# The q and k loads of an attention and MLP kernel moved from SyncE's DMA queue to GpSimd's, and two raw weight loads asked for at an earlier place

## The chip, the cores and the metric

One NeuronCore of a Trainium2 chip runs the whole program. The metric is device time in microseconds of one execution, as the median of three runs. The profile that is read below comes from one more execution, with the hardware profiler on, and its own time stands in the table beside its span.

## What is computed

The reference, cut to what matters:

```python
# q, k, v: (4, 12, 448, 64) fp32; cap: a scalar, 30
scores = cap * tanh((q @ k.T / sqrt(64)) / cap)
attn   = exp(scores - max) ; attn = attn / sum(attn)
x      = (attn @ v)                        # (4, 12, 448, 64) -> (1792, 768)
h      = relu(x @ w_in) ; x = (h * h) @ w_out          # first MLP, d_ff 2048
h      = x @ w_in2 ; x = (h * sigmoid(1.702 h)) @ w_out2   # second MLP
```

The MLP weights come as float64 and are used as 32-bit words, which the kernel makes itself from the raw bytes.

## The kernel before

All of it is `bounded_cap`; `any_cap` is a second version for a large cap and does not run here. The program is one long list of steps written in source order, and `in_order` (L1398) keeps that order on every engine, so each engine and each DMA queue works through its own fixed list.

**Attention.** The 48 heads are 24 pairs `(b, p)`; two pairs make a quad, of which there are 12. A quad takes four steps, one for each chunk of keys, and `attn_step(s)` (L901) writes step `s`, with `n, c = divmod(s, 4)` for quad `n` and chunk `c`. TensorE (PE) transposes q and k through the identity (`transposed`, L799), VectorE (DVE) splits them into a high and a low part (`prep_q`, `prep_k`), PE makes the scores (`scores`, L824), ScalarE (ACT) does tanh and exp (L847, L851), and PE multiplies with the values (`pv`, L853). The products with v of quad `n` begin in its own last step and end in the second step of quad `n + 1` (table `PV`). `take`, `invert` and `divide` (L872 to L892) normalize a quad, one to two quads later, and write it to the scratch tensor `xs` in DRAM through GpSimd's queue.

**The loads.** `attn_loads(s)` (L939) asks for q, k and v of later quads by the table `LOADS`: q of a quad 8 and 7 steps ahead of its first step, k 8 and 10 steps, v 2 steps.

```python
LOADS = ((8, "q", 0), (8, "k", 1), (7, "q", 1), (10, "k", 0), (2, "v", 0), (2, "v", 1))
KB, QB, VB = 4, 3, 4    # buffers for k, q and v, each of one pair
```

In `load_k` (L775) a pair's k is two transfers of 96 KB (the first 384 keys of each head, L779) and two of 16 KB (the last 64 keys, the tail, L781). `load_q` (L783) makes two transfers of 112 KB, `load_v` (L789) one of 192 KB and two of 16 KB. A quad is thus 4 transfers for q, 8 for k and 6 for v, 18 in all. All go out on SyncE's queue (SP, `Q_LOAD`), but for q of the first quad.

**The weights.** While attention runs, `weight_group` and `weight_slot` (L1030, L1042) turn the first `ATT_CHUNKS` pieces of raw weights into words: GpSimd's queue (POOL) loads raw bytes (`wraw`, L969, three buffers of the pool `l`), ACT and DVE join them (L981, L985), DVE makes sums (L1009 to L1012), and POOL stores four parts to the scratch tensors `wsa` or `wsb` (L1000). In each quad POOL issues two raw loads, four weight stores and two stores to `xs`; in the seventh, eighth and tenth quad also three loads of `x` slices back from `xs` (`x_slice`, L1166).

**The MLPs.** After the last quad PE runs the list `seq`, one product after another (L1147), with weights fetched by SP (`load_grain`, L1110) and split by ACT and DVE (L1123, L1124). `place["a"]`, called `k` in the loop, counts the products of the first kind. At place `w0 - 2` of the first list (`W_AT` 10, so place 8) `weight_group` lines up the next seven raw pieces, and from place 10 on `weight_slots` works through them. The three buffers of the pool `l` hold at that time the two `xl` tiles that `x_rest` reads in places 2 and 3 (`X_LATE`) and the tile `xo` of the last quad, which is divided and stored in places 4 and 5.

Of the kernel before, what the change touches and what calls it, by code (L numbers as in the profile page):

```python
# [677 lines left out]
def bounded_cap(ctx, tc, q, k, v, cap, w1, w2, w3, w4, out, over):  # L678

    nc = tc.nc  # L680
# [7 lines left out]
    TAIL = NCH - 1  # L688
# [8 lines left out]
    Q_LOAD = nc.sync  # L697
# [31 lines left out]
    def flush():  # L729

        now, later[:] = list(later), []
        for f in now:
            f()
# [32 lines left out]
    MAIN = TAIL * P  # L766
    pairs = [(b, p) for b in range(B) for p in range(NP)]
    quads = [pairs[n : n + 2] for n in range(0, len(pairs), 2)]
    raw, vst, prep, pps, sc, et, pvp = ({} for _ in range(7))

    def halves():
        for j in range(2):
            yield j, slice(64 * j, 64 * j + 64)

    def load_k(b, p):  # L775

        kt = raw[b, p, "k"] = kz[pairs.index((b, p)) % KB]
        for j in range(2):
            Q_LOAD.dma_start(out=kt[:, :TAIL, j], in_=k[b, 2 * p + j, :MAIN].rearrange("(p c) d -> p c d", c=TAIL))  # L779
        for j, r in halves():  # L780
            Q_LOAD.dma_start(out=kt[r, TAIL, j], in_=k[b, 2 * p + j, MAIN:])  # L781

    def load_q(b, p):  # L783
        qt = raw[b, p, "q"] = ld.tile([CP, NCH, 2, D], F32, tag="q", name="qt")
        queue = nc.scalar if (b, p) in quads[0] else Q_LOAD
        for j in range(2):
            queue.dma_start(out=qt[:, :, j], in_=q[b, 2 * p + j].rearrange("(p c) d -> p c d", c=NCH))

    def load_v(b, p):  # L789
        vt = vst[b, p] = vz[pairs.index((b, p)) % VB]  # L790
        h = slice(2 * p, 2 * p + 2)
        Q_LOAD.dma_start(
            out=vt[:, : 2 * TAIL].rearrange("p (h c) d -> p h (c d)", h=2),
            in_=v[b, h, :MAIN].rearrange("h (p c) d -> p h (c d)", c=TAIL),
        )
        for j, r in halves():
            Q_LOAD.dma_start(out=vt[r, 2 * TAIL + j], in_=v[b, 2 * p + j, MAIN:])

    def transposed(t, name, bank=None):  # L799
        if bank is None:  # L800
# [138 lines left out]
    def attn_loads(s):  # L939

        for d, f, i in LOADS:
            f = {"k": load_k, "q": load_q, "v": load_v}[f]
            m, at = divmod(s + d, NCH)
            if at == 0 and 0 <= m < len(quads) and (m or f == load_v):
                f(*quads[m][i])
# [79 lines left out]
    work = []  # L1025
# [4 lines left out]
    def weight_group(m):  # L1030

        now = [todo.pop(0) for _ in range(m)]
        loads = [(load, u) for load, join, sums in now for u in range(2)]
        work.extend(loads[:3])
        del loads[:3]
        for load, join, sums in now:
            for u in range(2):
                work.extend([(join, u), *loads[:1]])
                del loads[:1]
            work.append((sums,))  # L1040
# [21 lines left out]
    def weight_slots(k, m, n):  # L1062

        for _ in range(3 * n * k // m, 3 * n * (k + 1) // m):
            weight_slot()
# [23 lines left out]
    for l in range(2):  # L1089
        for c in range(2):  # L1090
            seq += [(l, c, "a", s, o) for s, o in a_products(l, c)]
            b = [(l, c, "b", s, d) for s in (1, 2, 6, 7, 4, 5, 3) for d in range(NX)]
# [10 lines left out]
    def load_grain(n):  # L1103
        if n >= len(grains):
            return
        u, h = grains[n]
        l, c, kind, s, i = seq[u]
        t = wload[n] = wf_p.tile([P, 4 * P], F32, tag="wf", name="wf")
        if kind == "a":
            Q_W.dma_start(out=t[:, : NX * P], in_=wsa[l][i, PLACE[s]])  # L1110
        else:
            Q_W.dma_start(out=t, in_=wsb[l][i, PLACE[s], :, 4 * P * h : 4 * P * (h + 1)])
# [21 lines left out]
    def product(u):  # L1134
        l, c, kind, s, i = seq[u]
        key = (l, c, kind, i, CHAIN[s])
        ps = bank(key) if s in (1, 5) else banks[key]
        ks = NX if kind == "a" else NJ
        for kk in range(ks):
            whi, wlo = wt[gpos[u] + kk // 4]  # L1140
            if kind == "a":
                f, at = forms[l, c, "a", s, 0], kk
            else:
                f, at = forms[l, c, "b", s, kk // 3], kk % 3
            hi, lo = f[:, 0, at, :], f[:, 1, at, :]
            for n, (a, r) in enumerate(((whi, hi), (whi, lo), (wlo, hi))):
                nc.tensor.matmul(  # L1147
                    ps[:, :S], a[:, kk % 4, :], r,
                    start=(s in (1, 5) and kk == 0 and n == 0), stop=(kk == ks - 1 and n == 2),
                    skip_group_check=True,  # L1150
                )
# [114 lines left out]
    def b_step(l, c, s, ch):  # L1266

        k0, n = CHUNKS[ch]
        g11, g12, g21, g22 = (gt[x][:, k0 : k0 + n] for x in ("11", "12", "21", "22"))

        def form(src):
            split_form((l, c, "b", s, ch), src, n)

        def put(o, x, y, op=ALU.subtract):
            later.append(lambda: v_.tensor_tensor(o, x, y, op))


        if s == 1:
            form(g11)
        elif s == 2:  # L1280
            form(g21)
            t = gt["t", ch] = wide("tl")[:, :n]
            put(t, g12, g11, ALU.add)
        elif s == 6:
            form(gt["t", ch])
            put(g11, g22, gt["t", ch])
        elif s == 7:
            form(g12)
            put(g21, g21, gt.pop(("t", ch)))
        elif s == 4:  # L1290
            form(g21)
        elif s == 5:
            form(g11)
        else:
            form(g22)
# [98 lines left out]
    def new_g():  # L1394
        for x in ("11", "12", "21", "22"):
            gt[x] = pool["g"].tile([P, NJ, S], F32, tag="g" + x, name="g" + x)
# [18 lines left out]
    for x in quads[0]:  # L1415
        load_k(*x)
        load_q(*x)
# [5 lines left out]
    for s in range(-6, NCH * len(quads) + 3):  # L1423
# [4 lines left out]
        attn_loads(s)  # L1428
        if held and held[0][0] <= s and s % NCH in RAW_AT:
            _, f, a = held.pop(0)  # L1430
# [31 lines left out]
    for u, (l, c, kind, s, i) in enumerate(seq):  # L1462
        if (kind, s, i) == ("a", 1, 0):
            new_g()
            place = {"a": 0, "b": 0}
        flush()
        product(u)
        first_b = ((6, NJ - 1), (2, NJ - 1), (3, NJ - 2))
        if kind == "a" and (s, i) in first_b:
            b_step(l, c, 1, first_b.index((s, i)))  # L1470
        if u == 0:
            hi, lo = wt[0]
            for n in range(3):
                b = pool["pb"].tile([P, 512], F32, tag="b", name="pb")
                nc.tensor.matmul(
                    b[:, :S], hi[:, 0, :], forms[0, 0, "a", 1, 0][:, 0, 0, :], start=True, stop=True
                )
        while split < min(gpos[u] + W_AHEAD + 1, len(grains)):
            if loaded <= split:
                load_grain(loaded)  # L1480
                loaded += 1
            split_grain(split)
            split += 1
            load_grain(loaded)
            loaded += 1
        nxt = (l, c + 1) if c == 0 else (l + 1, 0)
        order = (1, 2, 6, 7, 4, 5, 3)
        n = order.index(s) + 1
        if kind == "b" and nxt[0] < 2 and place["b"] == 14:
            x_step(*nxt, 0)  # L1490
        if kind == "b" and n < 7:
            b_step(l, c, order[n], i)
        now, soon[:] = list(soon), []
        after(u)
        for f in now:
            f()
        k = place[kind]
        place[kind] += 1
        if kind == "a":
            m = A_WORK.get((l, c), 0)  # L1500
            if (l, c) == (0, 0):
                for n in X_LATE.get(k, ()):
                    x_rest(n)
            elif k in X_LAST:
                x_step(l, c, 5 + X_LAST.index(k))
            w0 = W_AT if (l, c) == (0, 0) else 5
            if k == w0 - 2:
                weight_group(m)
            if w0 <= k < W_END:
                weight_slots(k - w0, W_END - w0, m)  # L1510
        else:
            (t0, t1), m = B_WORK.get((l, c), ((0, 0), 0))
            if m and k == t0:
                weight_group(m)
            if t0 <= k < t1:
                weight_slots(k - t0, t1 - t0, m)
            if nxt[0] < 2:
                if k >= 17:
                    x_step(*nxt, k - 16)
# [21 lines left out]
X_REST = (46, 50, 50, 50)  # L1541
X_LATE = {2: (4,), 3: (5,), 4: (6,), 5: (7,)}
W_AT = 10
RAW_AT = (0, 1, 2, 3)
LOADS = ((8, "q", 0), (8, "k", 1), (7, "q", 1), (10, "k", 0), (2, "v", 0), (2, "v", 1))
KB = 4
QB = 3
RAWQ = lambda nc: nc.gpsimd
W_END = 50
X_LAST = (1, 3, 5)  # L1550
W_AHEAD = 4
A_WORK = {(0, 0): 17 - ATT_CHUNKS, (0, 1): 7, (1, 0): 6}
B_WORK = {(0, 0): ((8, 14), 2), (0, 1): ((8, 14), 2)}
# [45 lines left out]
```

## Time and profile before

| | |
|---|---|
| median of three runs | 1082.67 us (1081.75 to 1083.28) |
| profiled execution | 1074.54 us, span of its instructions 1072.7 us |
| granted TensorE clock, mean | 0.998 |
| PE busy | 1044.3 us (97%) |
| DVE busy | 823.8 us (77%) |
| ACT busy | 686.4 us (64%) |
| POOL busy | 281.0 us (26%) |
| GpSimd's DMA queue (q0) | 122.32 MB, 34.7% of 16 engines |
| SyncE's DMA queue (q1) | 104.29 MB, 32.1% of 16 engines |

Attention fills the first 231 us of the span, the two MLPs the rest. The busy shares are averages over stages with different limits; a busy PE may be a PE that holds a long instruction. The chain of waits tells, followed back from the end, which piece of work the end stood on. A DMA's time "to landing" runs from its issue to the arrival of its last byte. Rows of SPq are the issues of SyncE's queue, and the length of such a row is the time that the queue spent on issuing.

### The profile page before, as it was taken

Reading aid. Unit: us, or ns where it says so; the run is one execution under the profiler, and the core shown is the slowest. Engines: PE = TensorE matmul, PEld = TensorE weight load, DVE = VectorE, ACT = ScalarE, POOL = GpSimd, SP = SyncE. Lnnn points to the kernel's source line nnn. Section 1 sums busy time; section 2 is a strip of 40 time slices with the busy share of each in tenths; the row PEclk is TensorE's granted clock in tenths of the full one; section 3 lists DMA queues with packets and bytes.
Section 4 is the critical chain, followed back from the end, with each engine's and each line's share of the span. In section 5 each row is a group of like instructions: output and inputs, shape, how many; then the busy total and the mean of one; then the engine's idle time right before and its main releaser. Section 6 shows DMA issues by size and latency. Waiting matters only on the chain.

```text
span 1072.7 us, 17090 instructions
## 1 busy us (share of the span) xinstructions
PE 1044.3 (97%) x5887; PEld 863.5 (81%) x5887; DVE 823.8 (77%) x1176; ACT 686.4 (64%) x1072; POOL 281.0 (26%) x423
## 2 busy tenths in 40 slices
PE   7989989998999999999999999999999999999997
PEld 4444444467999999999999999999899889999996
DVE  3686878876889886987898769888894985568854
ACT  5877869975767565667765647666555365565551
POOL 1322334223541022134302223341013400001033
PEclk9999999999999999999999999999999999999999
DMA  5898998956996487699945667996344643333443
GB/s 115 222 274 245 291 271 249 287 179 184 369 355 202 136 276 270 195 352 355 330 147 178 232 231 228 327 302 198 120 141 135 193 145 105 112 110 120 133 130 70
DMA packets 149504, 228.36 MB, mean 213 GB/s; under 512 B 65488, under 2 KB 102480, under 8 KB 149408
## 3 DMA queue, kind: packets, MB, share of 16 engines
q0 software_dynamic: 36800, 122.32, 34.7%
q1 hardware_dynamic: 110512, 104.29, 32.1%
q8 instruction: 48, 0.79, 0.3%
q10 hardware_dynamic: 2096, 0.57, 0.2%
q14 instruction: 48, 0.39, 0.1%
HBM read 166.53 MB, written 60.56 MB: 212 GB/s over the span
## 4 chain that ended last, share of the span: by engine, by line
PE 83%; DMA 8%; issue 5%; POOL 1%; DVE 1%; ACT 1%; SPq 0%; ACTq 0%; POOLq 0%; DVEq 0%
PE pa L1147 39%; PE pb L1147 32%; PE sps L834 4%; DMA vz<-in_v_dram 4%; PE vxps L867 2%; PE vyps L867 2%; PE vsps L867 2%; DMA qt<-in_q_dram 1%; DMA out_dram<-o 1%; DMA wraw<-in_moe_w_out_dram 1%; DMA xl<-ys 1%; PE qps L804 1%; POOL xs L892 0%; PE sps L804 0%; PE kps L804 0%
## 5 line engine op out<-in xcount | busy, mean ns | idle before, releaser
L1147 PE MATMUL pa<-form,wh 128*128 128x448 f32 x1536 | 439.5, 367 | 0.4 <-DVE form L1156 0.4
L1147 PE MATMUL pb<-form,wh 128*128 128x448 f32 x1152 | 329.5, 367 | 3.4 <-ACT pb L1367 2.5
L1147 PEld LDWEIGHTS pa<-form,wh 128*128 128x128 f32 x1536 | 288.3, 188 | 28.1 <-DVE form L1156 1.1
L1147 PE MATMUL pa<-form,wl 128*128 128x448 f32 x768 | 282.0, 367 | 1.4 <-DVE wl L1124 1.4
L1123 ACT ACTIVATE wh<-wf 128x384 fp32r<-128x384 f32 (+1 forms) x392 | 212.0, 562 | 79.5 <-DMA wf<-wsa 35.0
L1124 DVE TENSOR_TENSOR wl<-wf,wh 128x384 fp32r<-128x384 f32 (+1 forms) x392 | 227.7, 606 | 21.4 <-ACT wh L1123 21.0
L1147 PEld LDWEIGHTS pb<-form,wh 128*128 128x128 f32 x1152 | 216.0, 188 | 24.2 <-ACT pb L1367 2.9
L1147 PE MATMUL pb<-form,wl 128*128 128x448 f32 x576 | 211.1, 367 | 0.0
L1147 PEld LDWEIGHTS pa<-form,wl 128*128 128x128 f32 x768 | 144.2, 188 | 15.9 <-DVE wl L1124 2.8
L1337 POOL DMA_DIRECT2D out_dram<-o x92 | 57.7, 634 | 257.2 <-DVE o L1335 253.0
L1147 PEld LDWEIGHTS pb<-form,wl 128*128 128x128 f32 x576 | 108.2, 188 | 9.7
L1156 DVE TENSOR_TENSOR form<-g,form 128x1344 fp32r<-128x1344 f32 (+1 forms) x72 | 100.7, 1398 | 5.5 <-ACT form L1155 4.8
L847 ACT ACTIVATE e<-sps 128x896 f32<-128x896 f32 (+1 forms) x96 | 74.9, 823 | 33.5 <-PE sps L834 28.8
L1360 ACT ACTIVATE qu<-pb 128x448 f32<-128x448 f32 x88 | 47.4, 539 | 65.5 <-PE pb L1147 63.3
L985 DVE SCALAR_TENSOR_TENSOR wy<-wraw,sx 128x768 int32<-128x768 int32 (+1 forms) x68 | 61.7, 907 | 31.9 <-ACT sx L981 25.4
L851 ACT ACTIVATE e<-e,ecap 128x896 f32<-128x896 f32 (+1 forms) x96 | 85.9, 951 | 0.0
L1155 ACT ACTIVATE form<-g 128x1344 fp32r<-128x1344 f32 (+1 forms) x72 | 85.8, 1192 | 0.0
L834 PEld LDWEIGHTS sps<-qq,kk 64*128 64x128 f32 (+1 forms) x504 | 51.0, 191 | 33.9 <-ACT e L851 10.2
L834 PE MATMUL sps<-qq,kk 64*128 64x448 f32 (+1 forms) x504 | 76.9, 393 | 1.4 <-ACT kk L812 1.4
L981 ACT ACTIVATE sx<-wraw 128x768 f16<-128x768 bf16 (+1 forms) x68 | 69.6, 1024 | 4.4 <-DMA wraw<-in_moe_w_out_dram 3.0
L969 POOL DMA_DIRECT2D wraw<-in_moe_w_out_dram x72 | 53.9, 751 | 59.4 <-DVE wy L985 29.9
L867 PE MATMUL vxps<-e,vz 128*32 128x448 f32 x384 | 52.6, 550 | 8.4 <-DMA vz<-in_v_dram 8.4
(118 smaller groups left out, 1013.7 us busy)
## 6 DMA issues: line engine op xcount, KB each, us to landing
wf<-wsa SPq DMA_DIRECT2D x224, 192.0 KB, 3.9
wf<-wsb SPq DMA_DIRECT2D x168, 256.0 KB, 3.1
wraw<-in_moe_w_in_dram POOLq DMA_DIRECT2D x32, 766.5 KB, 8.2
wraw<-in_moe_w_out_dram POOLq DMA_DIRECT2D x48, 383.2 KB, 6.0
wsa<-wy POOLq DMA_DIRECT2D x32, 384.0 KB, 5.8
wsb<-wy POOLq DMA_DIRECT2D x24, 384.0 KB, 5.0
wsa<-ws POOLq DMA_DIRECT2D x16, 384.0 KB, 6.4
wraw<-in_moe_w_out_dram POOLq DMA_DIRECT2D x24, 255.5 KB, 5.9
```

Source lines behind the costliest of these rows:

```text
L834: nc.tensor.matmul(ps[:, u, :S], x, y, start=all(t[0] != u for t in todo[:n]), stop=all(t[0] != u for t in todo[n + 1 :]),)
L847: a_.activation(e, chunk(c, sc.pop((b, p, c)))[:, :, :S], AF.Tanh)
L851: a_.activation(e, e, AF.Exp, scale=ecap)
L867: nc.tensor.matmul(ps[32 * i : 32 * i + 32, :S], x, t, start=c == 0, stop=c == TAIL, skip_group_check=True,)
L981: a_.activation(z, words(BF16)[:, :, :, 2], AF.Copy)
L985: v_.scalar_tensor_tensor(y[:, : 2 * n].bitcast(I32), words(I32)[:, :, :, 0], 13, sx[:, : 2 * n], ALU.logical_shift_right, ALU.bitwise_or,)
L1123: a_.activation(x, src, AF.Copy)
L1124: later.append(lambda: v_.tensor_tensor(y, src, f32(x), ALU.subtract))
L1147: nc.tensor.matmul(ps[:, :S], a[:, kk % 4, :], r, start=(s in (1, 5) and kk == 0 and n == 0), stop=(kk == ks - 1 and n == 2), skip_group_c ...
L1155: a_.activation(f[:, 0, :n, :], src, AF.Copy)
L1156: later.append(lambda: v_.tensor_tensor(f[:, 1, :n, :], src, f32(f[:, 0, :n, :]), ALU.subtract))
L1337: nc.gpsimd.dma_start(out=out[b * S : (b + 1) * S, m * P + 32 * j : m * P + 32 * j + 32].rearrange("(c p) d -> p c d", p=32), in_=o[32 * j ...
```

## The change

From the third quad on, the 96 KB parts of k and all of q are issued by GpSimd's queue; the 16 KB tails of k and all of v stay on SyncE's. In the first list of the first MLP, `weight_group` is called at place 4 and the first two raw loads of that group go out at once there.

```diff
+    QK_LOAD, QQ_LOAD, V_LOAD = LOADQ(nc)
     def load_k(b, p):
         kt = raw[b, p, "k"] = kz[pairs.index((b, p)) % KB]
+        queue = Q_LOAD if (b, p) in quads[0] + quads[1] else QK_LOAD
         for j in range(2):
-            Q_LOAD.dma_start(out=kt[:, :TAIL, j], ...
+            queue.dma_start(out=kt[:, :TAIL, j], ...
...
     def load_q(b, p):
-        queue = nc.scalar if (b, p) in quads[0] else Q_LOAD
+        queue = nc.scalar if (b, p) in quads[0] else Q_LOAD if (b, p) in quads[1] else QQ_LOAD
...
     def load_v(b, p):
-        Q_LOAD.dma_start(
+        V_LOAD.dma_start(
...
-            if k == w0 - 2:
+            if k == (W_RAW if (l, c) == (0, 0) else w0 - 2):
                 weight_group(m)
+                if (l, c) == (0, 0):
+                    for _ in range(2):
+                        f, *a = work.pop(0)
+                        f(*a)
...
-RAW_AT = (0, 1, 2, 3)
+RAW_AT = 10
+LOADQ = lambda nc: (nc.gpsimd, nc.gpsimd, nc.sync)
+W_RAW = 4
```

`RAW_AT` is read only where raw loads are held back on SyncE's queue; here they go out on GpSimd's, so it plays no part. On PE, DVE and ACT the instructions stand in the same order before and after. They move on POOL and SP alone, at three places.

GpSimd's queue, one quad of attention, before: `wsa` are weight stores, `wraw` raw loads, `xs` the stores of a finished quad. DMASW0 to DMASW7 are eight semaphores that this queue's transfers take in turn, so that a transfer that waits for one waits for the transfer eight places ahead of it.

```order
L1000 DMA wsa_126<-wy 128x2x384 [waits DMASW4_49,DVE_49]
L969 DMA wraw<-in_moe_w_in_dram 128x6x1022 [waits DMASW5_49,Activation_49]
L892 DMA xs<-x_677 4x32x448 [waits DMASW6_49,DVE_49]
L892 DMA xs<-x_679 4x32x448 [waits DMASW7_49,DVE_49]
L969 DMA wraw<-in_moe_w_in_dram 128x6x1022 [waits DMASW0_49,DVE_49]
L1000 DMA wsa_126<-ws 128x2x384 [waits DMASW1_49,DVE_49]
L1000 DMA wsa_126<-wy 128x2x384 [waits DMASW2_49,DVE_49]
L1000 DMA wsa_126<-wt 128x384 [waits DMASW3_49,DVE_49]
```

The same stretch after the change (`qt` is q, `kz` is k; lines are three higher):

```order
L1003 DMA wsa_126<-wy 128x2x384 [waits DMASW6_49,DVE_49]
L972 DMA wraw<-in_moe_w_in_dram 128x6x1022 [waits DMASW7_49,Activation_49]
L895 DMA xs<-x_677 4x32x448 [waits DMASW0_49,DVE_49]
L895 DMA xs<-x_679 4x32x448 [waits DMASW1_49,DVE_49]
L790 DMA qt<-in_q_dram 112x4x64 [waits DMASW2_49,PE_49]
L790 DMA qt<-in_q_dram 112x4x64 [waits DMASW3_49]
L782 DMA kz_118<-in_k_dram 128x3x64 [waits DMASW4_49]
L782 DMA kz_118<-in_k_dram 128x3x64 [waits DMASW5_49]
L972 DMA wraw<-in_moe_w_in_dram 128x6x1022 [waits DMASW6_49,DVE_49]
L1003 DMA wsa_126<-ws 128x2x384 [waits DMASW7_49,DVE_49]
L1003 DMA wsa_126<-wy 128x2x384 [waits DMASW0_49,DVE_49]
L1003 DMA wsa_126<-wt 128x384 [waits DMASW1_49,DVE_49]
```

Two transfers of q and two of k stand behind the stores to `xs`, and two and two more follow the last weight store of the quad: 16 transfers in a quad where there were 8.

SyncE's queue, one quad of attention, before:

```order
L787 DMA qt<-in_q_dram 112x4x64 x2
L779 DMA kz_116<-in_k_dram 128x3x64 x2
L781 DMA kz_116<-in_k_dram 64x64 x2
L787 DMA qt<-in_q_dram 112x4x64 x2
L779 DMA kz_117<-in_k_dram 128x3x64 x2
L781 DMA kz_117<-in_k_dram 64x64 x2
L792 DMA vz_121<-in_v_dram 128x2x192
L797 DMA vz_121<-in_v_dram 64x64 x2
L792 DMA vz_122<-in_v_dram 128x2x192
L797 DMA vz_122<-in_v_dram 64x64 x2
```

And after the change:

```order
L784 DMA kz_116<-in_k_dram 64x64 x2
L784 DMA kz_117<-in_k_dram 64x64 x2
L795 DMA vz_121<-in_v_dram 128x2x192
L800 DMA vz_121<-in_v_dram 64x64 x2
L795 DMA vz_122<-in_v_dram 128x2x192
L800 DMA vz_122<-in_v_dram 64x64 x2
```

The two loads of v (`vz`) had twelve transfers of q and k in front of them in the quad, and now have four.

GpSimd's queue at the beginning of the first MLP, before (`xo` is the last quad's tile):

```order
L1203 DMA xl<-xs 128x3x448 x2
L892 DMA xs<-x_2537 4x32x448
L892 DMA xs<-x_2539 4x32x448
L892 DMA xs<-xo 4x32x448 x2
L969 DMA wraw<-in_moe_w_out_dram 128x2x1022 x4
L969 DMA wraw<-in_moe_w_out_dram 128x3x1022 x2
```

And after:

```order
L1206 DMA xl<-xs 128x3x448 x2
L895 DMA xs<-x_2537 4x32x448
L895 DMA xs<-x_2539 4x32x448
L972 DMA wraw<-in_moe_w_out_dram 128x2x1022 x4
L895 DMA xs<-xo 4x32x448 x2
L972 DMA wraw<-in_moe_w_out_dram 128x3x1022 x2
```

The two raw loads, of two transfers each, now stand ahead of the store of the last quad.

## Rows read from the trace of the kernel before

**Rows 1.** The page, part 4: chain that ended last, shares by line.

```profile
PE pa L1147 39%; PE pb L1147 32%; PE sps L834 4%; DMA vz<-in_v_dram 4%; PE vxps L867 2%; PE vyps L867 2%; PE vsps L867 2%; DMA qt<-in_q_dram 1%; DMA out_dram<-o 1%; DMA wraw<-in_moe_w_out_dram 1%; DMA xl<-ys 1%; PE qps L804 1%; POOL xs L892 0%; PE sps L804 0%; PE kps L804 0%
```

**Rows 2.** Timeline of PE in attention: start us, us, instructions [idle before <-releaser].

```profile
43.17 1.49 PE L834 MATMUL sps<-qq,kk 64*128 64x448 f32 x12
...
60.21 1.49 PE L834 MATMUL sps<-qq,kk 64*128 64x448 f32 x12
...
64.02 0.60 PE L804 MATMUL qps<-ident,qt 112*128 112x112 f32 x4
...
78.96 0.57 PE L867 MATMUL vxps<-e,vz 128*32 128x448 f32 x2 [3.16 <-DMA vz<-in_v_dram]
...
81.34 1.49 PE L834 MATMUL sps<-qq,kk 64*128 64x448 f32 x12
...
198.11 0.58 PE L804 MATMUL qps<-ident,qt 112*128 112x112 f32 x4 [1.01 <-DMA qt<-in_q_dram]
...
210.87 1.48 PE L834 MATMUL sps<-qq,kk 64*128 64x448 f32 x12
```

**Rows 3.** Waits of PE: line <- waited for: us, times, longest.

```profile
PE vxps L867 <- DMA vz<-in_v_dram: 8.4, 4, 3.5
```

**Rows 4.** Timeline of SyncE's queue, 45 to 70 us.

```profile
45.48 0.52 SPq L792 DMA_DIRECT2D vz<-in_v_dram  x1
...
51.44 4.47 SPq L779 DMA_DIRECT2D kz<-in_k_dram  x2
...
64.55 0.87 SPq L792 DMA_DIRECT2D vz<-in_v_dram  x1
...
67.94 1.96 SPq L792 DMA_DIRECT2D vz<-in_v_dram  x1
```

**Rows 5.** DMA, 43 to 205 us: queue shares, then issues, KB, us to landing.

```profile
q0 software_dynamic: 10372, 31.03, 59.5%
q1 hardware_dynamic: 38311, 11.58, 31.7%
...
wraw<-in_moe_w_in_dram POOLq DMA_DIRECT2D x13, 766.5 KB, 8.3
wsa<-wy POOLq DMA_DIRECT2D x16, 384.0 KB, 5.3
xs<-x POOLq DMA_DIRECT2D x18, 224.0 KB, 8.9
vz<-in_v_dram SPq DMA_DIRECT2D x19, 192.0 KB, 7.7
qt<-in_q_dram SPq DMA_DIRECT2D x32, 112.0 KB, 6.6
kz<-in_k_dram SPq DMA_DIRECT2D x32, 96.0 KB, 6.9
wsa<-ws POOLq DMA_DIRECT2D x8, 384.0 KB, 8.5
...
wsa<-wt POOLq DMA_DIRECT2D x8, 192.0 KB, 8.1
...
xt<-xs POOLq DMA_DIRECT2D x3, 224.0 KB, 8.9
```

**Rows 6.** Timeline of POOL in the quad that begins at 60.21 us.

```profile
63.82 1.42 POOL L892 DMA_DIRECT2D xs<-x  x2
```

**Rows 7.** Tile xs: issues on POOL, ns min/median/max, first and last start.

```profile
L892 POOL DMA_DIRECT2D xs<-x x22: 703/718/742, 46.9 to 230.6; - x22
```

**Rows 8.** Timeline of POOL at the beginning of the first MLP.

```profile
249.37 1.37 POOL L892 DMA_DIRECT2D xs<-xo  x2 [18.05 <-DVE xo L891]
250.72 2.95 POOL L969 DMA_DIRECT2D wraw<-in_moe_w_out_dram  x4
```

**Rows 9.** Timeline of ACT there.

```profile
261.58 0.77 ACT L981 ACTIVATE sx<-wraw 128x512 f16<-128x512 bf16 x1 [3.00 <-DMA wraw<-in_moe_w_out_dram]
```

**Rows 10.** Timeline of PE there.

```profile
263.21 0.67 PE L1147 MATMUL pb<-form,wh 128*128 128x448 f32 x2 [2.48 <-ACT pb L1367]
```

More of the change, by code (lines that the diff above doesn't have):

```diff
@@ L773, in halves @@
             yield j, slice(64 * j, 64 * j + 64)
+    QK_LOAD, QQ_LOAD, V_LOAD = LOADQ(nc)
     def load_k(b, p):
         kt = raw[b, p, "k"] = kz[pairs.index((b, p)) % KB]
+        queue = Q_LOAD if (b, p) in quads[0] + quads[1] else QK_LOAD
         for j in range(2):
-            Q_LOAD.dma_start(out=kt[:, :TAIL, j], in_=k[b, 2 * p + j, :MAIN].rearrange("(p c) d -> p c d", c=TAIL))
+            queue.dma_start(out=kt[:, :TAIL, j], in_=k[b, 2 * p + j, :MAIN].rearrange("(p c) d -> p c d", c=TAIL))
         for j, r in halves():
@@ L796, in load_v @@
         for j, r in halves():
-            Q_LOAD.dma_start(out=vt[r, 2 * TAIL + j], in_=v[b, 2 * p + j, MAIN:])
+            V_LOAD.dma_start(out=vt[r, 2 * TAIL + j], in_=v[b, 2 * p + j, MAIN:])
     def transposed(t, name, bank=None):
```

## The prediction, made before the changed kernel had run

> **What bounds the kernel now.** I read the chain of waits first, then the timeline of PE, then the queues that PE waited for. The chain [rows 1] is PE's own matmuls of the MLPs for some 71% of the span. Nothing that the change touches can shorten those, so its worth lies in what else stands on the chain, above all 4% for loads of v and 1% each for q and for raw weights.
>
> The timeline of PE [rows 2] shows what these shares cost. A quad begins with twelve score matmuls. From the beginning at 43.17 to the next at 60.21 no load is late, and the quad takes 17.04 us. The next begins only at 81.34, because at 78.96 PE had waited 3.16 us for v: this quad took 21.13 us. From 43.17 to 210.87 there are nine quads; nine of 17.04 would be 153.4 us, and they took 167.7. So **14.3 us** are lost to late loads in attention. The waits on v themselves add up to 8.4 us in four times [rows 3]; the rest is what follows a wait, since ACT runs dry behind PE and has to be filled again. One other wait, of 1.01 us, is for q, at 198.11 [rows 2].
>
> Why v is late stands in the rows of SyncE's queue [rows 4]. Between the v loads at 45.48 and at 64.55 it issued 18 transfers in 19.07 us, 1.06 us each and longer than the 17.04 us that a quad needs; the two k loads at 51.44 alone held it 4.47 us. So the queue falls behind, and v, which it issues last, pays. The second v of that quad went out at 67.94, and PE got it at 78.96.
>
> **Part by part.** *The loads leave SyncE's queue.* Eight of its 18 transfers go. At 1.06 us each the other ten take 10.6 us of a quad's 17.04, so the queue waits for buffers and is no longer behind. Already in the first such quad v would go out 8.5 us sooner (19.07 less 10.6), at 59.4 instead of 67.94. With the same 11.0 us on the way it is there at 70.4, and PE asks for it at 75.8 (78.96 less 3.16). The four waits on v go, with what follows them: the 14.3 us less the one late q, which I leave in at its full 1.0: **13.3 us**. The bounds: below it nothing, if another load takes over at the same places; above it the whole 14.3.
>
> *They arrive on GpSimd's queue.* Per quad it gets 4 transfers of q and 4 of k. The issue of one I price like an `xs` store, 0.71 us [rows 6, 7]: 5.7 us of POOL per quad. POOL computes nothing there, so this costs only if what it issues comes too late. What stands behind the new transfers are raw loads and weight stores, which ACT and DVE need about a quad later. The tightest is q itself. In the quad that begins at 60.21 the two `xs` stores are issued by 65.24 [rows 6], the first pair's q then by 66.7. If it takes as long to land as the slowest of its neighbours, 8.9 us for `xs` [rows 5], it is there at 75.6. PE transposes it one quad after 64.02, at 81.1 [rows 2]. That leaves 5.5 us. The second pair's q and all of k are needed only three steps later, in the quad's last step. I price this part at 0; the bounds come from the first two rivals.
>
> *How full GpSimd's queue gets.* Each of its transfers waits for the one eight places ahead, so at most eight are on their way. By the landing times [rows 5], a quad's two raw loads, four weight stores and two `xs` stores add up to 61.6 us, four of q and four of k to 54.0; 115.6 over eight is 14.5 us, under 17.04. In the three quads with loads of `x` slices, 26.7 us more (three of 8.9) make it 17.8 us, 0.7 too much: 2.1 us of lateness in all, against the 5.5 in hand. That is why I charge nothing.
>
> *Early loads.* The third quad's k and q may now go out beside the loads of the second, since SyncE no longer delays them. Each still waits until PE's transposes free its buffer. I price this at 0; if it held up the first scores, one late landing of q or k, under 7 us [rows 5], would be the most.
>
> *Raw weights at place 4.* Before, the four transfers went out at 250.72, behind the store of the last quad, for which POOL sat 18.05 us idle [rows 8]. ACT then waited 3.00 us for them [rows 9], and with it the copy that PE waited 2.48 us for [rows 10]. Now they stand ahead of that store and wait only for the two `xl` tiles that are read two places earlier. They need to come 3.0 us sooner and may come up to 18 us sooner. I take the **2.5 us**; the bounds are 0 and 2.5. The next raw load still waits for the store of `xo`, and ACT reaches it 2.5 us sooner than before; this may give some of it back.
>
> **The sum** is 13.3 + 2.5 = 15.8 us. Against the profiled execution that is 1074.54 - 15.8 = 1058.7. The median of the runs shown is 8.1 us longer than the profiled execution, for a reason that this trace does not show. I take the gain off the median: 1082.67 - 15.8 = **1066.9 us**.
>
> **Rivals.** *The DMA engines are full.* From 43 to 205 us the two queues together keep the sixteen engines busy for 91.2% of 162 us [rows 5], 147.7 us. Without the 13.3 us of waits the stretch is 148.7 us long. The same work would fill it to 99%, and then something must be late somewhere. For it speaks that every load lands slowly there. Against it: in the rows q1 moves 11.58 MB in 31.7% and q0 31.03 MB in 59.5%, so a byte costs 1.43 times as much on q1. The loads that move are 6.8 MB (32 of q at 112 KB, 32 of k at 96 KB); at q0's price they would take 9 us less of the engines' time (4.4 us a MB on q1, 3.1 on q0). Also, weight stores may slip behind attention. If the engines can be filled to 96%, the stretch takes 153.9 us, the gain in attention is 8.1, and the time 1082.67 - 8.1 - 2.5 = 1072.1; if they can be filled to 93% alone, it takes 158.8 us, and the time is 1077.0. The Trainium skill (DMA: Bandwidth & Descriptors, "Issuing engines are not separate DMA queues") states that transfers of all queues run on the same sixteen engines, and that spreading them saves only issue time. By that rule the engines' work does not shrink and the time is this rival's; the trace agrees in that both queues' shares add up to no more than the engines have, and the sum of the forecast does not need the opposite.
>
> *GpSimd's queue sets the pace.* With 16 transfers in a quad and eight on their way, a quad of 17.04 us needs a mean landing time of 8.5 us or less; by the rows it is 7.2 (115.6 over 16). If the q and k behind raw loads of 766.5 KB bring it to 10 us, which `xs` at 8.9 is not far from, a quad takes 20.0 us. Nine quads lose 26.6 us, the forecast's gain is gone, and the time is 1082.67 - 15.8 + 26.6 = 1093.5, **slower**. PE would then wait for q at `qps`, in every quad. The point from which it is slower than before is a mean of 9.4 us, where nine quads lose 15.8. Against it speak the 5.5 us in hand and that landing times shrink when the queue drains. The Trainium skill (SBUF — State Buffer, "SBUF: two separate sides") warns that a DMA issued by GpSimd is held up while VectorE runs a copy that uses both of its ports, such as one of fp32 within SBUF. By that rule this rival would be likelier; the 22 `xs` issues of this trace, all 703 to 742 ns beside a DVE that works most of the time, show no such hold-up [rows 7].
>
> *The change does not do what it says.* v stays late, since it still shares the engines with the raw loads: its 7.7 us to landing [rows 5] is not SyncE's issue time. Then only the 2.5 us are left, or nothing: 1080 to 1083.
>
> *More than the sum.* If the 8.1 us by which the median exceeds the profiled execution are also waits on loads, they go too: 1058.8.
>
> **How the numbers follow.** The forecast has 57%, its own range by the bounds 1066 (all 14.3 and 2.5) to 1071.5 (2.1 us of lateness and nothing from the raw weights); more than the sum 6%; full engines 19% (1072 to 1078); no effect 5%; GpSimd's pace 13%. A measurement of this kernel tells some 0.2%, 2.2 us, from no change. So faster is 57 + 6 + 19 = 82%, the same 5%, slower 13%. The range 1058 to 1078 holds the first three.
>
> **What would show it.** Right: quads of 17.0 us throughout, no wait of PE on `vz`, SyncE's v issued about 20 us ahead of its use, POOL busy nearly 12 us in a quad, no wait of ACT for `wraw` near 260 us. Wrong: PE waits at `qps` or at the transposes of k for DMA, POOL issues that stand behind each other without a wait on DVE, landing times on q0 over 9 us, or a v that still takes 10 us to land and is waited for.

## The result and the profile after

| | before | after |
|---|---|---|
| median of six runs each, one set | 1082.21 us (1076.87 to 1087.87) | 1066.73 us (1063.49 to 1067.69) |
| ratio, 95% interval | | 0.9855 (0.9821 to 0.9890) |
| profiled execution, span | 1074.54, 1072.7 us | 1065.05, 1063.3 us |
| PE busy, POOL busy | 1044.3, 281.0 us | 1040.3, 338.5 us |

The kernel is faster, by some 1.5%, and the time is the one forecast. But the two profiled executions are only 9.5 us apart, not 15.5. Their traces show which part of the forecast's sum is there.

The page, part 1, and from part 4 the chain by line, for the changed kernel:

```profile
PE 1040.3 (98%) x5887; PEld 863.7 (81%) x5887; DVE 823.7 (77%) x1176; ACT 685.1 (64%) x1072; POOL 338.5 (32%) x503
...
PE pa L1150 41%; PE pb L1150 33%; PE sps L837 6%; PE vyps L870 3%; PE vsps L870 3%; PE vxps L870 3%; DMA out_dram<-o 1%; DMA wf<-wsa 1%; DMA xt<-xs 1%; PE sps L807 1%; PE qps L807 1%; DMA wraw<-in_moe_w_in_dram 1%; ACT e L850 1%; PE kps L807 0%; DMA wsb<-wy 0%
```

Against [rows 1], the 4% for `vz` are gone. New are `xt<-xs` and `e` with 1% each, and also `wf<-wsa` and the raw weights of `w_in` with 1% each. The waits of PE (line, waited for: us, times, longest):

```profile
PE qps L807 <- DMA qt<-in_q_dram: 5.7, 1, 5.7
PE sps L837 <- ACT e L850: 5.6, 1, 5.6
```

The 8.4 us on `vz` [rows 3] are gone. The 5.7 us on q lie in the first 43 us and stood there before too. What is new is one wait of 5.6 us for ACT. The timeline of PE shows where:

```profile
43.19 1.49 PE L837 MATMUL sps<-qq,kk 64*128 64x448 f32 x12
...
60.23 1.49 PE L837 MATMUL sps<-qq,kk 64*128 64x448 f32 x12
...
77.26 1.49 PE L837 MATMUL sps<-qq,kk 64*128 64x448 f32 x12
...
111.33 1.49 PE L837 MATMUL sps<-qq,kk 64*128 64x448 f32 x12
...
128.36 1.49 PE L837 MATMUL sps<-qq,kk 64*128 64x448 f32 x12
...
132.18 0.60 PE L807 MATMUL qps<-ident,qt 112*128 112x112 f32 x4
138.42 2.61 PE L837 MATMUL sps<-qq,kk 64*128 64x448 f32 x12 [5.64 <-ACT e L850]
...
153.25 1.49 PE L837 MATMUL sps<-qq,kk 64*128 64x448 f32 x12
...
204.37 1.48 PE L837 MATMUL sps<-qq,kk 64*128 64x448 f32 x12
```

The quad that lost 4 us before, from 60.23, now takes 17.03. Of the nine quads eight take 17.0, and one, from 128.36 to 153.25, takes 24.9. Together they take 161.2 us, 7.8 more than 153.4, where before they took 167.7 [rows 2]. Attention has gained 6.5 us.

What ACT waited for stands in its timeline, first after, then before:

```profile
136.99 0.58 ACT L1177 ACTIVATE form<-xt 128x448 fp32r<-128x448 f32 x1 [8.71 <-DMA xt<-xs]
```

```profile
136.03 0.58 ACT L1174 ACTIVATE form<-xt 128x448 fp32r<-128x448 f32 x1 [1.90 <-DMA xt<-xs]
```

When that load was asked for stands in the timeline of POOL, again after and before:

```profile
108.59 0.71 POOL L1003 DMA_DIRECT2D wsa<-ws  x1 [1.63 <-DMA wraw<-in_moe_w_in_dram]
...
128.02 1.42 POOL L790 DMA_DIRECT2D qt<-in_q_dram  x2
129.43 0.56 POOL L1169 DMA_DIRECT2D xt<-xs  x1
```

```profile
127.42 0.55 POOL L1166 DMA_DIRECT2D xt<-xs  x1
```

`xt`, the first piece of the first x slice, is asked for at step 25 and used at step 27 (`X_AT`). It reached ACT at 136.0 before and at 137.0 after, almost the same moment. But ACT had come to it at 134.1 before, since the kernel was late by then, and comes to it at 128.3 now, 1.1 us before GpSimd's queue has even issued the load. So two things come together. The lateness that the change removes had covered part of this load's way. And the load has not come forward with the steps around it. The quad in which it is asked for begins at 117.21 before and at 111.33 now, so the load goes out 10.2 us into that quad before, and 18.1 us now. The row of PE for 117.21, before:

```profile
117.21 1.49 PE L834 MATMUL sps<-qq,kk 64*128 64x448 f32 x12
```

What holds the load back is GpSimd's queue. Before, that queue mostly waited for DVE to make the next words (`wy`); now it does so once, up to 45.3 us. The waits of POOL for `wy` from 43 to 129 us, before and after:

```profile
POOL wsa L1000 <- DVE wy L985: 47.6, 5, 12.8
POOL wraw L969 <- DVE wy L985: 15.8, 5, 6.1
```

```profile
POOL wsa L1003 <- DVE wy L988: 10.0, 1, 10.0
```

Each transfer of this queue waits for the one eight places ahead. With 8 transfers in a quad that was its own counterpart of the quad before. With 16 it is one of the same quad. So the weight store `ws` now waits for the quad's first raw load (both DMASW7 in the order rows of the change), as the row of 108.59 shows. The two issues of q just ahead of `xt` are only 1.4 us of the delay.

PE also started again at a low clock. The row of 138.42 shows 2.61 us instead of 1.49, and the granted clock from 138.4 to 143.5 us was 0.54, about the lower of the two levels, after PE had stood almost still from 132.7 to 138.4.

### The profile page after: what moved, and what is told of

It reads as the page before. It is cut to its first block, busy times and chain, and to the rows that moved or that the text cites. A ratio compares the mean times of both kernels' runs of the same rounds, so it can differ in the third digit from the quotient of the medians.

```text
span 1063.3 us, 17105 instructions
## 1 busy us (share of the span) xinstructions
PE 1040.3 (98%) x5887; PEld 863.7 (81%) x5887; DVE 823.7 (77%) x1176; ACT 685.1 (64%) x1072; POOL 338.5 (32%) x503
## 4 chain that ended last, share of the span: by engine, by line
PE 90%; DMA 4%; DVE 2%; ACT 1%; issue 1%; POOL 1%; ACTq 0%; DVEq 0%; POOLq 0%
PE pa L1150 41%; PE pb L1150 33%; PE sps L837 6%; PE vyps L870 3%; PE vsps L870 3%; PE vxps L870 3%; DMA out_dram<-o 1%; DMA wf<-wsa 1%; DMA xt<-xs 1%; PE sps L807 1%; PE qps L807 1%; DMA wraw<-in_moe_w_in_dram 1%; ACT e L850 1%; PE kps L807 0%; DMA wsb<-wy 0%
## 5 line engine op out<-in xcount | busy, mean ns | idle before, releaser
L1150 PEld LDWEIGHTS pa<-form,wl 128*128 128x128 f32 x768 | 144.2, 188 | 15.5 <-DVE wl L1127 2.6
L837 PEld LDWEIGHTS sps<-qq,kk 64*128 64x128 f32 (+1 forms) x504 | 51.8, 194 | 38.6 <-ACT e L850 13.9
L972 POOL DMA_DIRECT2D wraw<-in_moe_w_out_dram x72 | 53.1, 742 | 70.6 <-DVE wy L988 24.9
L1366 DVE SCALAR_TENSOR_TENSOR g<-pa,qu 128x448 f32<-128x448 f32 x64 | 39.7, 621 | 17.6 <-PE pa L1150 11.6
```

The lines of the kernel that those rows point to most:

```text
L837: nc.tensor.matmul(ps[:, u, :S], x, y, start=all(t[0] != u for t in todo[:n]), stop=all(t[0] != u for t in todo[n + 1 :]),)
L1150: nc.tensor.matmul(ps[:, :S], a[:, kk % 4, :], r, start=(s in (1, 5) and kk == 0 and n == 0), stop=(kk == ks - 1 and n == 2), skip_group_c ...
```

## The experiments

All stand beside runs of the kernel before on the same chip, whose median was 1078.8 us for e1 to e4, 1077.8 for e5 to e8, 1077.4 for e9 to e11 and 1077.1 for e12. Ratios are to those runs.

| run | median | ratio, 95% interval |
|---|---|---|
| e1 queue move alone | 1072.7 | 0.9938 (0.9911 to 0.9965) |
| e2 raw weights alone | 1072.9 | 0.9961 (0.9935 to 0.9986) |
| e3 change, `xt` early | 1062.7 | 0.9861 (0.9825 to 0.9898) |
| e4 change, more issues on SyncE | 1068.2 | 0.9908 (0.9874 to 0.9941) |
| e5 the change again | 1067.7 | 0.9906 (0.9869 to 0.9943) |
| e6 e3, x slices on SyncE | 1062.0 | 0.9846 (0.9799 to 0.9892) |
| e7 v moved, not q and k | 1061.8 | 0.9851 (0.9807 to 0.9894) |
| e8 change, k tails moved too | 1080.9 | 1.0036 (1.0010 to 1.0061) |
| e9 e7, `xt` early | 1061.4 | 0.9852 (0.9816 to 0.9887) |
| e10 q moved alone | 1063.3 | 0.9884 (0.9842 to 0.9926) |
| e11 e9, a chunk fewer | 1065.5 | 0.9876 (0.9838 to 0.9913) |
| e12 e2, v ahead of k | 1081.9 | 1.0024 (0.9994 to 1.0053) |

**e1 and e2: the two terms apart.** e1 puts back the raw weights, e2 the loads.

```
-            if k == (W_RAW if (l, c) == (0, 0) else w0 - 2):
+            if k == w0 - 2:
                 weight_group(m)
-                if (l, c) == (0, 0):
-                    for _ in range(2):
-                        f, *a = work.pop(0)
-                        f(*a)
```

```
-LOADQ = lambda nc: (nc.gpsimd, nc.gpsimd, nc.sync)
+LOADQ = lambda nc: (nc.sync, nc.sync, nc.sync)
```

> The queue move alone; the raw weights of the MLP are asked for at place 8 as before, with no transfer ahead of the work of place 10. If the two terms add (15.5 us measured, of which the waits of PE at pb fell by 2.3 us in the profiled runs), this kernel takes 1068.5 to 1069.5 us, and ACT waits some 3 us for wraw at the start of the MLP again. Rival: the early request is worth nothing, since the next load is late in its place: 1066.7 us.

> The early raw weights alone; q, k and v all on SyncE's queue as before. If the terms add: 1082.2 less 2.0 to 2.5, 1079.7 to 1080.2 us, with four waits of PE on vz as before. Rival: the early raw loads stand in front of the store of the last quad's x and delay it, and nothing is gained: 1082 us.

By the ratios e1 gains 6.7 us (3.8 to 9.6) and e2 4.2 (1.5 to 7.0); both terms are real, and their sum is near what e5 measures. Neither median lies where it was expected: e1 is 3 us above its range, and e2 7 us under its own, which had been taken from the 1082.2 of the first set. The traces give the terms sharper. From the last `xo` of attention on ACT to the product that waits for `pb`, the kernel before takes 33.2 us and e1 33.4, the change 31.6 and e2 31.3: the raw weights are worth 1.6 to 2.1 us. In the profile of e1 the nine quads take 163.4 us. In e2's, with the queues as before, they take 174.6, 6.9 us more than in the profile of before, with three waits on v:

```profile
PE vxps L870 <- DMA vz<-in_v_dram: 10.5, 3, 3.8
```

So how late v comes differs between executions of the same queues, and the profiled execution of before was the better of these two.

**e5: the change again.**

> The changed kernel once more, unaltered, so that the other variants of this call stand beside it in one set of runs, with a second profile. If the quad of 24.9 us in its first profile belongs to the kernel and not to one execution, ACT again waits 8 to 9 us for xt and the nine quads take 161 us; the time is 1063 to 1068 us. If it was an accident of one execution, the nine quads take 153.4 us, and the time of that execution is some 1057.

ACT waits 9.1 us for `xt`, and the nine quads take 162.4 us. The long quad belongs to the kernel, and `xt` goes out 19.4 us into its quad. With the queues of the change the nine quads lie between 161.2 and 163.4 us in three profiles. The gain in this set is 10.1 us (6.1 to 14.1).

**e3: the late load asked for sooner.** `xt` and `xu` of slice 0 at step 22; `xw` stays at step 25.

```
+        if s == 22:
+            x_slice(0, -1)
...
-        if step == 0:
+        if step < 0:
             get("t", left, 0)
             get("u", right, 0)
+        elif step == 0:
+            if i:
+                get("t", left, 0)
+                get("u", right, 0)
             get("w", right, NX)
```

> The changed kernel, with the loads xt and xu of the first x slice asked for at step 22 instead of 25; xw stays at 25. Theory: the one quad of 24.9 us in the changed kernel is late by 7.85 us because ACT waits 8.7 us for xt, a load that is asked for only two steps before its use; with the load 12 us earlier the quad takes 17.04 and the time is 1066.7 - 7.8 = 1058.9 us. Rival: the DMA engines are at their limit there, so another load (wraw or q) comes late in its place: 1063 to 1067 us.

No wait for `xt` is left, and the quad from 128.60 takes 17.3 us. But the nine quads take 159.6, in this execution only 1.6 less than in the change. From 146 us on DVE waits for weight stores to free their buffers, where in the change, in the same stretch, it did not. Timed, e3 takes 1062.7 us; 1058.9 was too low, and the rival's 1063 is nearer. No set holds both e3 and the change. By the ratios, 0.9861 against 0.9855 and 0.9906, a gain over the change is not settled. The waits of DVE in e3 from 145 to 205 us:

```profile
DVE wy L988 <- DMA wsa<-ws: 5.9, 3, 2.2
```

**e4: as many issues as before on SyncE's queue, few bytes.**

```
+    def extra(b, p):
+        if (b, p) not in quads[0] + quads[1]:
+            for j in range(2):
+                t = ld.tile([64, 16], F32, tag="dum", name="dum", bufs=8)
+                nc.sync.dma_start(out=t, in_=k[b, 2 * p + j, MAIN:, :16])
...
     def load_q(b, p):
+        extra(b, p)
...
+        extra(b, p)
         kt = raw[b, p, "k"] = kz[pairs.index((b, p)) % KB]
```

> The changed kernel, with eight small transfers a quad (64 rows of 64 bytes each, read by nobody) put on SyncE's queue where the eight of q and k stood, so that it again issues 18 in a quad; 32 KB a quad, against 832 KB that have left it. Theory A, the number of issues makes SyncE's queue late: at 1.06 us each 18 take 19.1 us, v is late again, and the time is 1076 to 1082 us. Theory B, what made the issues slow was the bytes and packets of q and k on the same engines: the extra issues take 0.5 to 0.6 us each, 10.6 + 4.6 = 15.2 us a quad, v stays in time, and the kernel takes 1066 to 1068 us.

The time is theory B's, but the issues are as long as theory A has them. The timeline of SyncE's queue shows 18 issues, from 69.40 to 88.02:

```profile
69.40 2.59 SPq L781 DMA_DIRECT2D dum<-in_k_dram  x4
72.52 3.79 SPq L792 DMA_DIRECT2D kz<-in_k_dram  x2
76.68 3.34 SPq L781 DMA_DIRECT2D dum<-in_k_dram  x4
80.13 1.22 SPq L792 DMA_DIRECT2D kz<-in_k_dram  x2
...
83.90 1.43 SPq L804 DMA_DIRECT2D vz<-in_v_dram  x1
85.42 2.55 SPq L809 DMA_DIRECT2D vz<-in_v_dram  x2
88.02 2.60 SPq L781 DMA_DIRECT2D dum<-in_k_dram  x4
```

That is 1.03 us for each in this quad, even with most of the bytes gone. (The three issues left out are those of the first v.) The queue is at its limit, and v is late once, by 3.1 us at 114 us; that quad loses some 7 us. For the rest it keeps up, and the time is that of e5. This late v takes the place of `xt`: PE and ACT come later by what the quad has lost, ACT waits 1.2 us for `xt` instead of 8.7, and no long quad follows. So the time that e4 has in common with e5 does not mean that the 18 issues cost nothing. They just fill the queue; with the bytes of q and k in them it is over the limit.

**e7 and e10: other loads moved.** In e7 (the first of the two edits) v of the first two quads stays on SyncE's queue.

```
-LOADQ = lambda nc: (nc.gpsimd, nc.gpsimd, nc.sync)
+LOADQ = lambda nc: (nc.sync, nc.sync, nc.gpsimd)
...
+        queue = Q_LOAD if (b, p) in quads[0] + quads[1] else V_LOAD
```

```
-LOADQ = lambda nc: (nc.gpsimd, nc.gpsimd, nc.sync)
+LOADQ = lambda nc: (nc.sync, nc.gpsimd, nc.sync)
```

> q and k stay on SyncE's queue; v of the quads from the third on moves to GpSimd's (six of 18 transfers, 0.45 MB a quad against 0.83 MB of the change); raw weights early as in the changed kernel. Theory A, what made v late is its place behind the q and k in SyncE's queue: v is no longer waited for, SyncE issues 12 in 12.7 us, and the time is that of the change, 1066 to 1068 us. Theory B, what counts is the bytes that move to GpSimd's queue, where one costs 3.1 us a MB instead of 4.4: about half of the gain of moving q and k, 1069 to 1073 us, with waits of PE on loads left.

> The changed kernel with k put back on SyncE's queue; only q goes to GpSimd's (four transfers a quad, 12 in all there, 14 on SyncE's). By the count of issues alone, 14 at 1.06 us are 14.8 us, v is in time, and GpSimd's queue is emptier than in the change: 1060 to 1066 us. But in e7 SyncE took 1.4 us for each of its 12 issues and was never done with a quad's; if its issues stretch until the queue is full whatever their number, then v, which stands last, is late again: four waits on vz of some 8 us, 1072 to 1080 us.

By the medians either serves at least as well as the change, and e7 is faster than both theories had it. In e7, with half the bytes moved, no wait on v is left, and GpSimd's queue has 14 transfers in a quad instead of 16. There `xt` keeps its place. It goes out 10.2 us into its quad, as before, though the lateness of v is gone as in the change. Its timelines of PE, POOL and ACT:

```profile
111.37 1.49 PE L838 MATMUL sps<-qq,kk 64*128 64x448 f32 x12
```

```profile
121.58 0.56 POOL L1170 DMA_DIRECT2D xt<-xs  x1
```

```profile
132.43 0.58 ACT L1178 ACTIVATE form<-xt 128x448 fp32r<-128x448 f32 x1 [4.13 <-DMA xt<-xs]
```

ACT still waits 4.1 us, as the load takes 10.8 us here, and the quad takes 19.9 us instead of 24.9. This tells the two causes apart: some 3 us of lateness at `xt` come without any delay of its issue, and the other 5 go with GpSimd's queue.

But SyncE's 12 issues do not take 12.7 us. Its timeline from one quad's loads to the next:

```profile
77.32 2.20 SPq L790 DMA_DIRECT2D qt<-in_q_dram  x2
79.56 1.50 SPq L782 DMA_DIRECT2D kz<-in_k_dram  x2
81.10 1.32 SPq L784 DMA_DIRECT2D kz<-in_k_dram  x2
82.52 3.37 SPq L790 DMA_DIRECT2D qt<-in_q_dram  x2
85.94 3.94 SPq L782 DMA_DIRECT2D kz<-in_k_dram  x2
89.92 3.44 SPq L784 DMA_DIRECT2D kz<-in_k_dram  x2
93.46 1.26 SPq L790 DMA_DIRECT2D qt<-in_q_dram  x2
```

Twelve take 16.1 us, 1.35 each. The price of an issue is not a constant of the queue. e10 lands where the count of issues put it, though v is late once, by 3.1 us, as in e4; with 12 transfers in a quad, `xt` goes out 11.6 us into its quad.

**e12: the order alone.** 

```
-LOADS = (..., (10, "k", 0), (2, "v", 0), (2, "v", 1))
+LOADS = (..., (2, "v", 0), (2, "v", 1), (10, "k", 0))
```

> All of q, k and v on SyncE's queue as before, the raw weights early as in e2; only the order of one step is changed: the two loads of v stand ahead of the first pair's k instead of behind it, so four issues fewer are in front of them. Theory A, v is late for its place behind the others in a queue that is never empty: v goes out some 4 us sooner, the waits of 3.1 to 3.8 us on vz in e2 go, and the time is 1062 to 1068 us although nothing moved to GpSimd's queue. Rival, the queue itself has too many issues for a quad (18 at 1.06 us): then k, behind v now, falls back by 2 us a quad, and after some quads PE waits for k or q instead: 1072 to 1080 us.

The rival is right, at a time above its range. PE does not wait for v any more, but for k and q, and the time is not under that of before:

```profile
PE kps L807 <- DMA kz<-in_k_dram: 12.5, 5, 5.1
PE qps L807 <- DMA qt<-in_q_dram: 8.7, 2, 5.7
```

So v was not late for its place in the list. The list as a whole is longer than a quad, and whatever stands behind pays.

**e8: more on GpSimd's queue.** 

```
-            Q_LOAD.dma_start(out=kt[r, TAIL, j], in_=k[b, 2 * p + j, MAIN:])
+            queue.dma_start(out=kt[r, TAIL, j], in_=k[b, 2 * p + j, MAIN:])
```

> The changed kernel with the four k tails of a quad (16 KB each) on GpSimd's queue as well, so 20 transfers a quad there instead of 16. Rival of the prediction, GpSimd's queue sets the pace: 115.6 us of landing times plus four of 5.1 make 136 us, over eight 17.0 us a quad and 20.3 us in the quads with x slices; each quad then loses what waits for that, 1070 to 1080 us. If the queue has room, 1066 to 1068 us; SyncE then issues six transfers in a quad and no load of v is late.

The gain is gone, and the time is just above the range of the rival. POOL asks for `xt` at 136.38, 7 us later than in the change and 24.7 us into its quad, and ACT waits longer, as its timeline shows. Yet the DMA engines are less busy than in any other kernel here (43 to 205 us, queue: packets, MB, share of 16 engines):

```profile
143.55 0.58 ACT L1177 ACTIVATE form<-xt 128x448 fp32r<-128x448 f32 x1 [12.68 <-DMA xt<-xs]
```

```profile
q0 software_dynamic: 13254, 35.21, 73.1%
q1 hardware_dynamic: 7179, 3.78, 9.6%
```

At 82.7% it is not the engines that are short. It is GpSimd's queue. With 12 or 14 transfers in a quad `xt` goes out 10 to 12 us into its quad, with 16 (the change, e1 and e5) after 18 to 19, and with 20 after 25. In e4, also with 16, a quad of PE is late just there, and the queue has caught up to 13.

**e6, e9 and e11: which limit is left.** e6 is e3 with the nine x slice loads on SyncE's queue, e9 is e7 with e3, e11 is e9 with `ATT_CHUNKS` 9 instead of 10.

```
-            Q_PUT.dma_start(out=t, in_=xs[b, k0 + i])      # e6, in x_slice
+            Q_LOAD.dma_start(out=t, in_=xs[b, k0 + i])
```

> The kernel with the early x loads (e3), and in addition the nine loads of x slices on SyncE's queue. In e3 the quads from 145 us on still take 18 to 20 us, since DVE waits for weight stores (wsa<-ws, 2.15 us in one place) and PE for DVE. Theory Q: GpSimd's queue, eight transfers on their way, is what is short there; nine transfers fewer at 6 us over eight give back 6.8 us, and the time is 1056 to 1058 us. Theory B: the DMA engines, 91% busy, are short; the same bytes then come as late: 1062 to 1063 us.

> v moved instead of q and k (e7), and xt and xu of the first x slice asked for at step 22 (e3). In e7's profile ACT still waits 4.1 us for xt in the quad that begins at 128.40; with that gone by the early load alone 1061.8 - 4 = 1058 us. If the engines, 95% busy in e7, are what is left, another load is late in its place: 1061 to 1063 us.

> e9 with nine weight chunks in attention instead of ten; the tenth is done with the first MLP's own (eight there instead of seven). A chunk is 1.5 MB of raw loads and 1.3 MB of stores, 2.9 of 43 MB that pass in the stretch. Theory B, in e3, e6 and e9 the full DMA engines set what is still late in attention: with 6 to 7% less to move the nine quads come near 153.4 us and the time is 3 to 5 us under e9's, unless the MLP takes it back, where DVE is 82% busy and PE waits for nothing. Rival: the first MLP needs that chunk before it is there, and PE waits for wf: slower than e9.

e6 is at theory B's time, 1062.0. Its slices land after 9.1, 10.3 and 7.5 us instead of 6.4, 5.7 and 6.4; DVE's waits for `wsa<-ws` between 40 and 215 us fall from 6.9 in e3 to 2.5 us, and a wait of 4.0 us for ACT's `form` is new. Which limit this is, e6 does not tell. e9's median is at the rival's time too, no better than e7. But its profile has the shortest attention of all. The nine quads take 154.4 us, 1.0 over the ideal:

```profile
43.67 1.49 PE L838 MATMUL sps<-qq,kk 64*128 64x448 f32 x12
...
198.07 1.48 PE L838 MATMUL sps<-qq,kk 64*128 64x448 f32 x12
```

```profile
q0 software_dynamic: 13317, 36.54, 70.4%
q1 hardware_dynamic: 32534, 8.72, 26.2%
```

This is its best execution of six. And it did it with the engines 96.6% full, so full engines alone need not hold up attention. e11 has less to move and is no faster: in its profile, of its slowest execution, PE waits 1.8 and 3.4 us for q inside attention. Theory B's forecast for it fails. What makes other executions of e9 up to 9 us longer than its best stays open. e9 has the shortest median and, with 1055.8 us, the shortest profiled execution of the kernels here. It beats the kernel before clearly. Its median is 5 to 6 us under the change's two, but no set holds both, the change's ratio in its first set, 0.9855, is e9's, and the intervals of e5, e7 and e9 overlap. So against the change it is not settled.

## Why the prediction was right, and where not

**The loads leave SyncE's queue: 13.3 us predicted, 6.5 found.** The mechanism is right. Before, the second v in [rows 4] went out at 67.94; the same load, the eighth of its kind, now goes out here:

```profile
54.08 0.59 SPq L795 DMA_DIRECT2D vz<-in_v_dram  x1
```

This is 13.9 us sooner (I had said 8.5), and no v is waited for. That a list of 18 issues is longer than a quad is shown by e12, where the lateness moves to k and q; in e4 18 mostly small ones just fill it. The detail was too simple: I took 1.06 us for each issue that stays, and e7 shows 1.35. One other load took over. In e9, where GpSimd's queue has 14 transfers in a quad and `xt` is early, the nine quads take 13.3 us less than the 167.7 of before, in its best execution: that is the gain predicted.

**How full GpSimd's queue gets: "2.1 us of lateness in all, against the 5.5 in hand", charged at nothing; 7.8 found.** This is the step that failed, in two ways. I compared the lateness with the slack of q, and the load that paid was `xt`. Where it keeps its place, it has 6.7 us from its issue to ACT's use (121.58 to 128.3 in e7), and it takes 6.6 to 10.8 (e5 and e7; 8.6 before). ACT's wait of 1.90 us for it stood in the trace of before, and I did not ask what that wait becomes when PE and ACT come 6 us sooner. And the lateness itself was too small: by the quad in front of the first x slice GpSimd's queue was already 7.9 us behind (18.1 us into the quad against 10.2). The sum of landing times over eight was not at fault; by the medians of the change it is 15.0 us a quad. But such an average under 17.04 does not show that each transfer goes out in its place. The sign of being wrong that I had named, issues of POOL without a wait on DVE, is there. So the change already has a part of the rival "GpSimd's queue sets the pace", and e7, e10 and e8 show how it grows with the number of transfers. e3 shows that the load `xt` is where it costs, and that most of the price is taken over by the weight stores on the same queue when `xt` goes out early (1.6 us won of 7.8 in its profile). My bound "nothing, if another load takes over at the same places" was the right kind of bound, with no name in it.

**q and k on GpSimd's queue, priced at 0: right for q and k.** PE waits for neither after 43 us. POOL's busy time from 43 to 205 us rises from 59.4 to 105.1 us, 4.8 us a quad where I said 5.7. The slack was thinner than it looked: e8 adds four small transfers and the rival "GpSimd's queue sets the pace" is there in full, though its wait is at `xt` and at DVE, not at `qps`. The Trainium skill (SBUF — State Buffer, "SBUF: two separate sides") warns that an issue of GpSimd's is held up while DVE runs a copy that uses both of its ports. The change issues two of q in 1.42 to 1.45 us beside a busy DVE, as the row of 128.02 shows; no run here shows a hold-up, and none was made to test for one.

**The engines are full: not what held the change.** In the change the two queues take 88.6% of the engines from 43 to 205 us, against 91.2% [rows 5], and e9 reaches 96.6% with an attention that is late by 1.0 us. The Trainium skill (DMA: Bandwidth & Descriptors, "Issuing engines are not separate DMA queues") states that another queue saves only issue time. The traces agree in that the queues' shares never add up to more than the engines have. But issue time on one queue is what the change was about, and the move was worth 6.5 us.

**Raw weights: 2.5 us predicted, 1.6 found.** ACT does not wait for `wraw` any more, POOL issues it 14.6 us sooner than before [rows 8], 6.5 of which are attention's, and the product waits 0.82 us instead of 2.48 [rows 10], since `wf` is late next. The timelines of POOL, ACT and PE after:

```profile
236.09 1.49 POOL L972 DMA_DIRECT2D wraw<-in_moe_w_out_dram  x2 [11.27 <-DVE form L1159]
```

```profile
251.18 0.53 ACT L1126 ACTIVATE wh<-wf 128x384 fp32r<-128x384 f32 x1 [3.68 <-DMA wf<-wsa]
```

```profile
255.11 0.68 PE L1150 MATMUL pb<-form,wh 128*128 128x448 f32 x2 [0.82 <-ACT pb L1370]
```

The next term, 0.9 us at `qu`, which I had not charged, falls to 0.3.

**The sum.** The traces give 6.5 in attention and 1.6 at the start of the MLP, 8.1 of the 15.8 predicted; the other 1.4 us of the 9.5 come later, in MLP stretches that the change does not touch and that differ by more between single executions. That the median nevertheless fell by 15.5 has a reason that I had left open: the profiled execution of before was 8 us under the median, and in e2's profile v costs 6.9 us more. The second set of runs puts the gain at 10.1. So the forecast of 1066.9 was right in part by luck, through two errors that offset each other: 7.8 us not charged for `xt`, and a lateness of v before that was larger in other executions than in the one profile I had. The first is shown; the second rests on e2's profile and the medians, and it is not shown that it makes up the whole difference.

## What to carry to other kernels

When a change removes a wait, ask of every load behind it when it lands and when its user would now come, and add the differences that become positive; a short wait in the trace of before is a candidate. When transfers are added to a queue, look up which transfer each one now waits for: an average that fits in the period does not show that a load keeps its place. A load needs a lead longer than its landing time on that queue, and moving few transfers (six of 18 in e7, four in e10) leaves the receiving queue more room. Take the lateness of loads from several executions before it is priced: it varied from 14 to 21 us here under the same queues.

## What was not expected of the hardware

SyncE's issues stretch: in a quad, 12 took 1.35 us each in e7, where the engines are 95.3% busy, 18 took 1.03 in e4 (91.7%), and 18 took 1.06 before (91.2%).

In MLP stretches where PE waits for nothing and the granted clock is 1.00, the same products run at two paces. From one row to the next but one, three matmuls take 0.62 us in one stretch of the kernel before, and 0.61 in the same part of e1:

```profile
880.22 0.57 PE L1147 MATMUL pa<-form,wh 128*128 128x448 f32 x2
...
880.84 0.57 PE L1147 MATMUL pa<-form,wh 128*128 128x448 f32 x2
```

```profile
872.63 0.57 PE L1150 MATMUL pa<-form,wh 128*128 128x448 f32 x2
...
873.24 0.57 PE L1150 MATMUL pa<-form,wh 128*128 128x448 f32 x2
```

From the product that waits for `pb` to the end, the profiles take 809.5 us (before), 808.2 (the change), 805.2 (e2) and 803.6 (e1). This is some 6 us between single executions, in a stretch that the edits leave alone; what sets the pace stays open.
